# Delta-rule attention and a gelu MLP on one core: all operations but the products of zeros, in an order found anew

## The chip, the core and the metric

The kernel runs on one core of a Trainium2 chip. Five engines with queues of their own do the work: TensorE (PE, matmuls; PEld is its weight loads), VectorE (DVE), ScalarE (ACT), GpSimd (POOL), and SyncE (SP), which here only issues transfers. ACT and POOL issue some transfers too. The metric is device microseconds of one execution. The profile is one execution taken by the hardware profiler; a run's time is that of the core from start to end.

## What is computed

For 4 batches of 8 heads, a state of 48 by 48 is carried over 768 tokens; its outputs, 384 wide per token, go through an MLP with gelu:

```python
for t in range(S):                       # S = 768, B = 4, H = 8, D = 48
    kt, vt, bt = k_n[:, :, t], v[:, :, t], beta[:, :, t, None]
    y[:, :, t] = einsum('bhd,bhde->bhe', q[:, :, t], state)
    v_old = einsum('bhde,bhd->bhe', state, kt)
    state = state + bt[:, :, :, None] * einsum('bhd,bhe->bhde', kt, vt - v_old)
...
x = y.transpose(0, 2, 1, 3).reshape(3072, 384)
h = x @ w_in                             # 384 x 2048
out = gelu_tanh(h) @ w_out               # 2048 x 384
```

`k_n` is k divided by its norm plus 1e-6. Inputs and output are float32; the kernel works in bf16 with float32 accumulation.

## The kernel before, in words

**Tiling.** The sequence is cut into 12 chunks of 64 tokens. Two batches lie side by side on the 128 partitions, so a chunk has two units, numbered u = 2c and 2c + 1, each with 8 head slots. Within a chunk the recurrence is solved with matrices: a unit needs the inverse of a triangular matrix of 64 by 64 per head, and the chunk's state then goes on to the next chunk.

**Stages of a unit** (function `prep`, L469). Keys, scaled keys and queries are cast to bf16 (`kc`, `kb`, `qb`). They are transposed, on PE (`T`, `Tc`, `Tb`, `Tk`, `Tq`, evicted by `kT...`) or by a transfer that SP issues (`turn`, L510). Products of transposed keys (`GM`, `G2`, `G`, `GQ`, L521) are masked by DVE (`ln`, `wp`, L525). The inverse is found in five rounds: the start value is written into block-diagonal tiles (`X10`, `X11`), and each round i is a product `A` (L566, 8 matmuls of 128 by 128 by 64 or less), an update on DVE (`rt`, L578: two times identity plus the product), a second product `B`, and an eviction into the block-diagonal tiles. That eviction has three forms: two half copies (`bde`), a half and a scaled full copy (`bdf`), or one full copy on ACT or DVE with two half copies behind it, mostly on POOL (`xi`, then `bdc`, L608). The update has a second form: an identity product `J` on PE ahead of the accumulating product (`C`), and a plain eviction (`rj`) that ACT can do.

**Stages of a chunk** (`chain`, L611). With the state of the chunk before: `K` and `Q` (L639), `R` on DVE, `U` (the inverse times the residual, L662), its eviction `Un`, the state's update `S` and `Sn`, the output `O` (L687), its eviction `On`, and a transpose by PE (`X`, `xT`) or by a transfer (`turnx`, L704).

**The MLP of a chunk** (`mlp`, L708). 16 up products of three matmuls each (`up0` to `up15`, L716), four of them to an ACT gelu over 1024 columns (`gelu0` to `gelu3`, L720); then for each of two blocks of 128 tokens four down products of four matmuls (`down00` to `down13`, L727), an eviction (`Z0`, `Z1`) and stores (`out`, L736 and L739). The weights come in four transfers that POOL issues, `w1.0`, `w1.1` (L440), `w2.0`, `w2.1` (L442), 768 KB each.

**Products of zeros.** `warm_up` (L397) declares 70 products of 128 by 128 by 512 of a tile of zeros (`fill`, L400). Their results are read by nobody.

**What sets the order.** No scheduler runs when the kernel is built. Every operation is declared with the engines that may do it, with the buffers that it reads and writes, and with an `alt` mark where another form does the same. The text `ORDER` (L17 to L117) is one sequence over all engines; each word names an operation, behind a colon the engine (the first one declared, where none is given) and behind @ the PSUM bank. `Flow.order` (L160) cuts it into the queues of the five engines; an operation that is declared and not named is left out. `Flow.emit` (L198) puts in the waits on semaphores that the buffers need. So each engine runs its words strictly in the text's order, and a waiting word holds up all behind it on its engine. Raw q, k and v have three buffers each (`NR`), so the load of chunk c waits for the readers of chunk c - 3; the tokens' bf16 tiles have six.

Of the kernel before, what the change touches and what calls it, by code (L numbers as in the profile page):

```python
# [21 lines left out]
fill46@0 J1.1@0 fill22@1 fill64@2 Tc.1@1 fill12@2 betaT0@3 fill63@4 Tc.0@2 fill60@4 fill9@5 fill56@4 sq.0b:d sum.0a sum.0b tabS pow.0a
kTc.1:a betaA010 betaA001 pow.0b betaA011 betaA000 epsb:d eps.0a:d nsq.0a:g inv.0a eps.0b:d nsa.0b inv.0b triwpm0:d bdz0:d ib.0b:d triwpm2:d
upone0 sq.1:a sum.1 ib.0a:g kb.0:g bdz1:g kb.1:g betaT1@3 Tb.0@1 kTc.0:d betaN111 betaN110 Tb.1@4 fill25@2 kTb.0:a pow.1 eps.1:g nsa.1
kTb.1:d GM.0@6 GM.1@4 J2.0@2 fill16@1 betaN101 two:d betaN100 inv.1 ib.1:g kb.2:g ln.0 kb.3:d wpm.0 ln.1 ladj16:d wpm.1 qb.0:a fill36@3
# [4 lines left out]
X10.3:g bdc30.0:g X11.2:g qb.3:g bdf20.1:a bdf21.1:a C3.1 rj3.1:a A1.3@0 GQ.1@4 fill1@1 fill45@2 wqa.1 A4.0@1 B3.1@2 fill55@3 Tq.3@3 A1.2@4  # L30
fill41@5 rt4.0 sum.2 rt1.3 B4.0@1 wqa.0 bdf30.1:a bdf31.1:a A4.1@5 fill14@0 rt4.1 B4.1@5 fill20@0 bdf40.0:a rt1.2 pow.2 bdf41.0:a bde41.1:a
A5.0@2 B1.3@4 bde40.1:d rt5.0 kTq.3:d B1.2@0 bde10.3:a xi1.2:a R0a.0:d eps.2:g bdz5:g wqb.0 A5.1@5 B5.0@2 rt5.1 kc.4:d bde11.3:d B5.1@3
bdf50.0:a qb.2:a bdc11.2:g bdc10.2:g R0b.0:g Tq.2@5 A2.2@0 bde51.1:d rt2.2 wqb.1 nsq.2:g bde50.1:a bdf51.0:a A2.3@4 U.0@2 tabG Un.0:a rt2.3
# [4 lines left out]
gelu3.0 bdf50.3:a gelu2.0 bdf51.3:a kc.7:a down00.0@2 down01.0 sum.3 turn.5 X11.4:g wp.4 vs.1:d X10.4:d G2.5@0 S.0@6 A1.4@3 v2.01 v2.10
v2.11 q3.00 q3.01 q3.10 q3.11 k4.01 k4.10 k5.10 k4.00 k4.11 down02.0 ln.5 pow.3 eps.3:g nsq.3:g Sn.0:a bde50.2:a bde51.2:a rt1.4 inv.3 G.5@0
K.1@6 wp.5 X11.5:g X10.5:g ib.3:g kb.7:g R.1 qb.7:g B1.4@3 down10.0@4 down11.0 bde11.4:a bde10.4:a A1.5@5 GQ.2@0 A2.4@3 U.1@6 down03.0 rt1.5  # L40
rt2.4 Un.1:a wpq.2 B2.4@3 B1.5@5 xi2.4:a Q.1@6 S.1@0 O.1 down12.0 qb.6:g kb.6:g Z0.0:d bdc21.4:d bdc20.4:g A3.4@3 sq.4:g bdf10.5:a Sn.1
On.1:a turn.7 bdf11.5:a X.1@2 down13.0 xT.1:a rt3.4 sum.4 A2.5@5 B3.4@3 rt2.5 up0.1@6 up1.1 G.7@0 Z1.0:a bdf30.4:a bdf31.4:a B2.5@5 up2.1
A4.4@4 G2.7@2 up3.1 turn.6 q4.00 q4.10 q4.01 out11.0 q5.10 bde21.5:a bde20.5:a gelu0.1 wp.7 rt4.4 ln.7 up8.1@0 A3.5@5 B4.4@4 up9.1 G2.6@2
G.6@6 pow.4 eps.4:g rt3.5 ln.6 nsa.4 inv.4 ib.4:d wp.6 bdf40.4:a bdf41.4:a up10.1 B3.5@5 up11.1 up4.1@2 up5.1 A5.4@4 up6.1 bdf30.5:a
bdf31.5:a X11.7:g X10.7:g A4.5@5 A1.7@6 up7.1 X10.6:d rt5.4 X11.6:g kc.9:g q4.11 rt4.5 B5.4@7 A1.6@4 kb.8:g qb.8:g k5.11 v3.01 k5.00 k5.01
gelu2.1 kc.8:a gelu1.1 xi5.4:a v3.00 q5.01 turn.8 v4.01 v3.11 vs.2:g bdc51.4:g bdc50.4:g qb.9:g sq.5:g kb.9:g q5.11 k6.01 q5.00 turn.9 k6.00
k6.10 v3.10 k6.11 rt1.7 B4.5@5 up12.1@0 up13.1 up14.1 B1.7@2 rt1.6 B1.6@4 K.2@6 bde41.5:a bde40.5:d A5.5@5 down10.1@3 bde11.7:d rt5.5
bde11.6:a bde10.6:a bde10.7:a R.2 B5.5@5 A2.6@4 up15.1 A2.7@2 down00.1@6 bdf50.5:a bdf51.5:a gelu3.1 rt2.6 rt2.7 sum.5 B2.6@7 U.2@4
bdf20.6:a Un.2:a B2.7@2 bdf20.7:d down01.1 down11.1 bdf21.6:d bdf21.7:d down12.1 G2.8@4 Q.2@0 A3.7@2 ln.8 rt3.7 A3.6@7 O.2 On.2:a S.2@4
B3.7@2 pow.5 X11.8:g eps.5:g X10.8:g bde30.7:a bde31.7:a nsa.5 down02.1 G.8@0 rt3.6 B3.6@7 Sn.2 down03.1 bde31.6:a A4.7@2 X.2@4 wp.8 inv.5  # L50
rt4.7 A1.8@5 down13.1 rt1.8 Z0.1:a bde30.6:a xT.2:a B4.7@2 A4.6@7 Z1.1:d rt4.6 G2.9@0 G.9@4 ln.9 wp.9 B1.8@3 xi4.7:a qb.10:a ib.5:g kb.11:g
qb.11:g kc.10:d kb.10:g bdc41.7:g bdc40.7:g X11.9:g vs.3:g X10.9:g bdf10.8:a bdf11.8:a up8.2@6 B4.6@2 bde41.6:a bde40.6:a up9.2 up4.2@0
up10.2 up11.2 A5.7@4 gelu2.2 up5.2 up6.2 A5.6@5 sq.6:d rt5.6 rt5.7 sum.6 up7.2 up0.2@2 K.3@6 B5.7@4 B5.6@5 R.3 k7.01 k7.00 k7.10 out11.1
k7.11 q6.01 v4.11 turn.10 q6.10 out00.0 kc.12:g kc.11:g turn.11 sq.7:g gelu1.2 up1.2 A2.8@0 up2.2 A1.9@1 up3.2 up12.2@6 up13.2 bde50.7:d
rt2.8 rt1.9 bde51.7:a bdf50.6:a bdf51.6:a U.3@4 up14.2 B2.8@0 gelu0.2 Un.3:a B1.9@1 Q.3@2 up15.2 bde11.9:a bde21.8:a gelu3.2 pow.6 eps.6:g
nsq.6:g bde10.9:d sum.7 pow.7 kc.14:g bde20.8:a O.3 On.3:d inv.6 A2.9@1 down00.2@4 ib.6:d rt2.9 down01.2 G.10@2 G2.10@6 wp.10 ln.10 down02.2
B2.9@5 down10.2@1 A3.8@0 down11.2 G2.11@6 S.3@2 rt3.8 X11.10:g X10.10:g kb.12:g ln.11 bde20.9:a kc.13:a bde21.9:a B3.8@5 bdf30.8:a bdf31.8:a
kb.13:g X10.11:g X11.11:g A3.9@0 down12.2 down13.2 k8.00 q6.00 v4.10 q6.11 qb.12:a qb.13:g turnx.3 v4.00 k8.01 k8.11 turn.12 k8.10 rt3.9
Sn.3 A4.8@5 rt4.8 B3.9@0 A1.10@6 eps.7:g vs.4:g G.11@2 down03.2 wp.11 Z0.2:d rt1.10 Z1.2:a bdf30.9:a bdf31.9:a B4.8@5 bde41.8:a bde40.8:a
up12.3@0 up13.3 A1.11@2 A4.9@3 rt4.9 up14.3 up15.3 out11.2 q7.01 turn.13 q7.00 out00.2 v5.01 v5.10 v5.00 q7.11 v6.10 q7.10 v5.11 gelu3.3  # L60
rt1.11 up0.3@6 B1.10@3 B4.9@5 A5.8@4 up1.3 K.4@0 up2.3 up3.3 bde41.9:d rt5.8 R.4 bde40.9:a bdf10.10:a A5.9@2 bdf11.10:a up4.3@4 gelu0.3
# [729 lines left out]
```

## Time and profile before

| what | us |
|---|---|
| runs, three | 262.08, 264.64, 266.80 |
| median of the runs | 264.64 |
| the profiled execution, first to last instruction (no other time of it is listed) | 261.9 |
| PE busy in it | 243.3 |
| DVE busy | 208.7 |
| ACT busy | 189.7 |
| POOL busy | 140.6 |
| first MLP product on PE starts at | 40.08 |

The page gives the span in 40 slices of 6.5 us; a digit is the busy share in tenths. Busy PE is not PE at its peak, since matmuls overlap; what a kind of product costs is read from dense stretches of the chain, not from the mean of one.

### The profile page before, as it was taken

Reading aid. Unit: us, or ns where it says so; the run is one execution under the profiler, and the core shown is the slowest. Engines: PE = TensorE matmul, PEld = TensorE weight load, DVE = VectorE, ACT = ScalarE, POOL = GpSimd, SP = SyncE. Lnnn points to the kernel's source line nnn. Section 1 sums busy time; section 2 is a strip of 40 time slices with the busy share of each in tenths; the row PEclk is TensorE's granted clock in tenths of the full one; section 3 lists DMA queues with packets and bytes.
Section 4 is the critical chain, followed back from the end, with each engine's and each line's share of the span. In section 5 each row is a group of like instructions: output and inputs, shape, how many; then the busy total and the mean of one; then the engine's idle time right before and its main releaser. Section 6 shows DMA issues by size and latency. Waiting matters only on the chain.

```text
span 261.9 us, 12280 instructions
## 1 busy us (share of the span) xinstructions
PE 243.3 (93%) x5481; PEld 189.0 (72%) x5481; DVE 208.7 (80%) x346; ACT 189.7 (72%) x305; POOL 140.6 (54%) x216
## 2 busy tenths in 40 slices
PE   5788869999999899979999989999999999999994
PEld 1356657777878768857887877787977878878672
DVE  4699996998999999949998979799999878665100
ACT  4878886879969867947986866887847858856260
POOL 7668563687986998575165462669433522011000
PEclk9979999999999999989999999999999999999999
DMA  4869999789986988993768969568976611001422
GB/s 89 148 128 154 194 186 179 139 158 170 151 154 131 139 158 159 161 166 72 142 121 161 175 122 149 102 121 111 161 144 86 120 33 33 5 3 33 91 64 60
DMA packets 118741, 31.87 MB, mean 122 GB/s; under 512 B 112800, under 2 KB 117920, under 8 KB 118688
## 3 DMA queue, kind: packets, MB, share of 16 engines
...
q0 software_dynamic: 2880, 3.15, 7.3%
...
q14 instruction: 10, 0.08, 0.1%
...
## 4 chain that ended last, share of the span: by engine, by line
PE 75%; SPq 10%; DMA 6%; DVE 5%; issue 2%; ACT 1%
PE ps L727 24%; PE ps L716 21%; PE ps L566 18%; SPq L431 10%; DMA qraw<-in_q_dram 6%; PE ps L521 4%; PE ps L639 3%; PE ps L662 2%; PE ps L687 2%; DVE wp L525 1%; PE ps L674 1%; DVE sq L454 1%; DVE tok L484 1%; DVE rl L578 1%; SPq L406 0%
## 5 line engine op out<-in xcount | busy, mean ns | idle before, releaser
L716 PE MATMUL ps<-xT,W 128*128 128x256 bf16 x576 | 77.4, 273 | 0.4 <-ACT xT L338 0.2
L338 ACT ACTIVATE bd<-ps 64x512 bf16<-64x512 f32 x108 | 62.2, 588 | 17.6 <-PE ps L566 16.3
L727 PE MATMUL ps<-W,gT 128*128 128x384 bf16 x384 | 73.2, 329 | 0.0
L720 ACT ACTIVATE gT<-ps 128x1024 bf16<-128x1024 f32 x48 | 48.4, 1020 | 12.4 <-PE ps L716 12.0
L716 PEld LDWEIGHTS ps<-xT,W 128*128 128x128 bf16 x576 | 50.1, 98 | 6.4 <-ACT xT L338 0.5
L578 DVE TENSOR_TENSOR rt<-ps,two 128x512 bf16<-128x512 f32 x68 | 45.4, 684 | 6.6 <-PE ps L566 6.0
L727 PEld LDWEIGHTS ps<-W,gT 128*128 128x128 bf16 x384 | 33.7, 98 | 18.5 <-issue 0.7
L608 POOL COPY bd<-xi 64x256 f32<-64x256 f32 x46 | 19.0, 413 | 50.3 <-ACT xi L338 44.7
L555 POOL TENSOR_SCALAR_AFFINE_SELECT bd<-ln 64x512 bf16<-64x512 bf16 x43 | 29.7, 692 | 20.3 <-DVE ln L525 15.6
L525 DVE CAST_PREDICATED wp<-mup,ps 128x1024 bf16<-128x1024 uint16 (+1 forms) x26 | 28.3, 1090 | 2.6 <-PE ps L521 2.5
L457 POOL TENSOR_TENSOR nrm<-nrm,half 128x16 f32<-128x16 f32 x9 | 26.2, 2908 | 5.7 <-DVE nrm L455 5.5
L566 PE MATMUL ps<-rt,bd 128*128 128x64 bf16 x576 | 27.9, 194 | 0.3 <-DVE rt L578 0.3
L566 PE MATMUL ps<-wp,bd 128*128 128x64 bf16 (+1 forms) x576 | 27.3, 188 | 0.7 <-POOL bd L555 0.5
L578 DVE TENSOR_TENSOR rl<-ps,two 128x384 bf16<-128x384 f32 (+1 forms) x48 | 22.9, 483 | 5.4 <-PE ps L566 4.8
L338 DVE CAST bd<-ps 64x512 bf16<-64x512 f32 x37 | 25.0, 680 | 2.5 <-PE ps L566 2.1
L566 PEld LDWEIGHTS ps<-wp,bd 128*128 128x128 bf16 x576 | 23.6, 98 | 4.3 <-POOL bd L555 0.9
L566 PEld LDWEIGHTS ps<-rt,bd 128*128 128x128 bf16 x576 | 23.2, 98 | 4.2 <-DVE rt L578 0.8
L566 PE MATMUL ps<-rl,bd 128*128 128x64 bf16 x384 | 18.5, 193 | 2.1 <-DVE rl L578 2.1
L525 DVE CAST_PREDICATED ln<-mlo,ps 128x512 bf16<-128x512 uint16 x24 | 16.3, 682 | 4.9 <-PE ps L521 4.7
L566 PE MATMUL ps<-ln,bd 128*128 128x48 bf16 (+1 forms) x384 | 18.1, 188 | 1.0 <-DVE bd L338 1.0
L338 ACT ACTIVATE xi<-ps 128x512 bf16<-128x512 f32 x24 | 14.0, 593 | 6.5 <-PE ps L566 6.3
L566 PEld LDWEIGHTS ps<-rl,bd 128*128 128x128 bf16 x384 | 15.1, 98 | 4.8 <-DVE rl L578 3.1
...
## 6 DMA issues: line engine op xcount, KB each, us to landing
...
W<-in_moe_w_in_dram POOLq DMA_DIRECT2D x2, 768.0 KB, 10.6
W<-in_moe_w_out_dram POOLq DMA_DIRECT2D x2, 768.0 KB, 19.1
kT<-tok SPq DMA_TRANSPOSE x19, 4.5
...
```

The lines of the kernel that those rows point to most:

```text
L338: return e.activation(out, in_, ACT.Copy) if e is nc.scalar else e.tensor_copy(out, in_)
L431: lambda e, P, n=n, a=a, y=y, xs=xs, view=view: e.dma_start(raw[n][s][hf(a), :, :].rearrange("p (xg y) d -> p xg y d", y=2)[:, xs, y, :], ...
L457: if e is nc.scalar else e.tensor_tensor(nr[:, 1, hx], nr[:, 0, hx], half[:, hx], ALU.pow), reads=[nrn, "half"] + ["one", "roots"] * (c < ...
L521: ins = e.matmul(o, kT[s][r, y, g, hf(a)], kT[s][r, z, g, hf(a)])
L525: return e.copy_predicated(out.rearrange("p (x g) t -> p x g t", x=2), mask[:, 0:wd].bitcast(U16).unsqueeze(1).unsqueeze(1).to_broadcast([ ...
L555: A(("pool", "dve"), op(f"X1{a}"), lambda e, P, src=ln[m][hf(a), :, :], dst=bd[b_][hf(a), :, hf(a)], a=a: e.affine_select(out=dst, in_=src ...
L566: ins = e.matmul(P(name)[:, C * h + cs.start:C * h + cs.stop], bd[b_][:, h, :], rhs[:, h, cs], **kw)
L578: A(("dve",), op(f"rt{i}"), lambda e, P, i=i, cs=cs, cn=cn, r_=r_: e.tensor_tensor(r_[:, :, cs], P(ps(f"A{i}")).rearrange("p (h t) -> p h ...
L608: A(("pool", "dve"), op(f"bdc{i}{a}"), lambda e, P, src=xi[i_][hf(a), :, :], dst=bd[b_][hf(a), :, hf(a)]: e.tensor_copy(dst.bitcast(F32), ...
L716: ins = e.matmul(P(ph)[:, 256 * f:256 * f + 256].rearrange("p (x t) -> p x t", x=2), W1[:, j, 128 * (i + f):128 * (i + f) + 128], x_[:, :, ...
L720: A(("act",), f"gelu{i // 4}.{c}", lambda e, P, i=i, ph=ph: e.activation(g_[:, i:i + 4, :], P(ph).rearrange("p (f t) -> p f t", f=4), ACT. ...
L727: ins = e.matmul(P(po)[:, 0:DM], g_[:, f, 128 * b:128 * b + 128], W2[:, f, :], start=(f == 0), stop=(f == FC - 1))
```

## The change

Only the text `ORDER` differs. It had 1750 words and has 1701. By queue, PE had 686 and has 652, DVE 346 and 356, ACT 309 and 308, POOL 212 and 190, SP 197 and 195. The 31 words `fill...` are gone, so no product of zeros is left; the memset of their tile (`wz`) stays. All other work is there, in one of its forms, in a new sequence, with new engines and banks:

- the update with an identity product (`J`, `C`, `rj`) is used for 1 round instead of 4; `rt` for 119 instead of 116;
- the eviction by `xi` and `bdc` is used for 17 rounds instead of 30, `bde` for 64 instead of 55, `bdf` for 39 instead of 35;
- PE transposes unit 7 instead of unit 4, which is now transposed by a transfer (`turn.4`); the number of transfers of this kind stays at 19, that of `turnx` at 7;
- the masks of unit 0 and 1's query products are done by DVE (`wpq`) instead of ACT and POOL (`wqa`, `wqb`);
- the weights' four transfers, next to each other before, stand apart;
- of the four last stores two are issued by SP and two by ACT, before three and one.

The start of both texts, and the places that the prediction speaks of:

```diff
 ORDER = """
-k0x0.10:s k0x0.01:s k0x1.01:s k0x1.10:s beta00:s k1.00 k1.01 k1.10 k1.11 beta11:s q0.00 q0.01 q0.10 q0.11 v0.00 v0.01 v0.10 v0.11 wz:d
-fill23@0 tmplz:d pad0:g pad4:g tmpl0 k0x0.00:a k0x1.00:a tmpl1 fill54@1 k2.00 k2.01 k2.10 k2.11 q1.00 q1.01 q1.10 q1.11 v1.00 v1.01 v1.10
...
-qb.1:g X11.1:g fill47@6 A1.0@7 rt1.0 fill52@6 Tk.2@6 kTk.2:d B1.0@3 C1.1 w1.0 w1.1 w2.0 w2.1 GM.3@6 GM.2@4 kTq.0:a bde11.0:a bde10.0:d C2.0
...
+pad3:g half ident:g tmplz:d pad4 pad2:g one bdz5:g pad0:g tmpl0 tmpl1 triln0:d triwpm3:d epsb:g identf ladj32:d k0x0.01 pad1:g mmlo:d
+k0x0.10:a k0x1.10 k0x1.01:a k0x1.11:a two:d k0x1.00 triln1:d triwpm0:d k0x0.11 bdz0 sq.0b:d k0x0.00:a sq.0a:d mlo0 kc.1:g sum.0b sum.0a
+k1.01 beta01:a beta00:a betaT0@3 betaN000 beta10 bdz1:g k1.11 betaN010 betaN011 tabS pow.0b pow.0a k1.00 eps.0b betaN001 k1.10 k2.01 k2.00
...
+GM.1@4 ln.1 X11.1 triwpm1 nsa.1 inv.1 betaT1@0 sq.2 sum.2 triln3 betaA100 betaA101 betaA111 A1.0@1 rt1.0 B1.0@1 q1.10 betaA110 ib.1 ladj16
...
+q2.10 k3.00 bdz2:g q2.11 Tq.2@5 Tq.3@4 kTq.3 k3.11 GQ.0@6 B3.1@0 X10.3 kTq.2 w1.0 bdf30.1 k4.00 A4.0@1 rt4.0 bdf31.1 q4.10 GM.2@2 ln.2 X11.3
+A1.3@4 rt1.3 q2.01 B4.0@1 bde41.0 A4.1@0 rt4.1 kb.4:g bde40.0 wpm.2 k4.10 Tq.1@5 B1.3@4 w1.1 X10.2 B4.1@0 bdf40.1 A5.0@1 X11.2 A1.2@2 rt5.0
...
+v1.11 up2.0 up3.0 v1.10 triwpm4 bdf31.3:d wpq.3 B3.2@0 A4.3@1 rt4.3 up4.0@6 qb.4:g turn.4 qb.5:g tabG gelu2.0 w2.0 up12.0@4 up13.0 up5.0
...
+up7.11 up14.11 up15.11 down00.11@0 down10.11@1 gelu1.11 down01.11 down02.11 gelu3.11 out00.10 down03.11 down11.11 down12.11 down13.11 Z1.11
+Z0.11:d out01.11 out00.11 out10.11:a out11.11:a
 """
```

More of the change, by code (lines that the diff above doesn't have):

```diff
@@ L22 @@
[L22 to L25, printed above, removed]
@@ L30 @@
[L30 to L33, printed above, removed]
@@ L38 @@
[L38 to L61, printed above, removed]
@@ L70 @@
-up10.4 A2.13@0 up11.4 gelu3.4 G2.14@2 rt2.13 ln.14 gelu2.4 B5.11@6 B2.13@7 bde51.11:a bde21.13:a bde50.11:a G.14@0 G2.15@2 bde20.13:d ln.15
-wp.14 up0.4@4 up1.4 up2.4 B3.12@2 up3.4 U.5@6 A3.13@3 up4.4@0 up5.4 up6.4 up7.4 gelu0.4 xi3.12:d rt3.13 inv.8 X11.15:d X11.14:g X10.15:g
-X10.14:g A1.14@3 B3.13@2 rt1.14 bde31.13:d Un.5:a Q.5@6 gelu1.4 S.5@4 O.5 G.15@0 bdc31.12:g bdc30.12:g ib.8:g kb.17:g out11.3 q8.10 v6.01
-v7.10 v6.00 q8.00 q8.11 k10.00 q9.01 k9.10 k9.01 k9.11 v7.00 bde30.13:a qb.17:a turn.17 On.5:a Sn.5 wp.15 down00.4@3 A4.13@2 down01.4
@@ L82 @@
-A3.15@0 K.7@2 A4.14@1 up14.5 up15.5 up0.6@4 rt3.15 kc.19:d R.7 A1.16@0 up1.6 up2.6 up3.6 A1.17@2 B3.15@3 gelu3.5 xi3.15:a rt1.16 B1.16@0
-rt4.14 B4.14@1 down00.5@6 rt1.17 B1.17@7 down01.5 bdf40.14:a bdf41.14:a xi1.16:a sq.10:g bdc31.15:d bdc11.16:g bdc10.16:g bdc30.15:d sum.10
-A4.15@1 A5.14@3 down02.5 down03.5 rt5.14 bde10.17:d B5.14@0 A2.16@3 down10.5@2 down11.5 k11.10 kc.22:g pow.10 qb.19:g gelu0.6 bde11.17:a
-bdf50.14:a bdf51.14:a rt2.16 rt4.15 B2.16@3 bde20.16:d Z0.5:d bde21.16:a B4.15@1 down12.5 A2.17@0 bde41.15:a bde40.15:a turn.18 q10.00
@@ new lines @@
+down13.0 Z1.0 B2.5@0 bde21.5 bde20.5:d q4.11 B3.4@3 up0.1@1 up1.1 k5.11 turn.6 G2.6@4 bde30.4 kc.8:g ln.6 bde31.4 G.7@6 up2.1 up3.1 q4.00
+q4.01 qb.9:a up8.1@4 up9.1 A4.4@0 wp.7 up10.1 up11.1 A3.5@3 qb.8:g gelu0.1 rt4.4 gelu2.1 rt3.5 B4.4@0 bde41.4:d bde40.4 v2.00 up4.1@6 up5.1
+B3.5@1 bdf30.5 X10.6 G.6@2 wp.6 up12.1@4 bdf31.5 q5.00 A5.4@0 rt5.4 up6.1 up7.1 A4.5@1 rt4.5 k5.00 gelu1.1 k5.10 X11.6 q5.01 A1.6@2 A1.7@3
+q6.11 B5.4@0 bde51.4 up13.1 B4.5@1 bdf40.5 up14.1 v4.10 rt1.6 B1.6@2 kb.9:g bde50.4:d q6.00 rt1.7 down00.1@6 sq.5:g sum.5 kc.11:g turn.8
@@ new lines @@
+ib.5:g v5.10 kb.11:g X.2@4 B4.6@5 xi4.6 down03.1 bdc40.6 rt4.7 B4.7@0 bde41.7 xT.2:d up4.2@4 up5.2 up6.2 up7.2 k7.11 gelu1.2 rt1.8 B1.8@1
+bde11.8 q6.10 bdc41.6:d A5.6@7 out00.0 bde40.7:d A5.7@0 rt5.7 v4.00 up0.2@2 up1.2 G.9@4 rt5.6 k6.10 bde10.8:d B5.6@7 up2.2 xi5.6 up8.2@0
+up3.2 up9.2 up10.2 A2.8@7 v4.01 up11.2 v3.11 kb.10:g v4.11 wp.9 sq.6 X10.9 vs.3 turn.10 gelu0.2 kc.13 sum.6 k8.11 v5.00 rt2.8 X11.9 A1.9@4
+k8.00 qb.11:g turn.11 gelu2.2 Z0.1 k8.10 k8.01 rt1.9 B5.7@5 bde50.7 bde51.7 k7.01 bdc51.6 down10.2@2 down00.2@3 B1.9@4 bdf10.9 k7.00 bdf11.9
@@ new lines @@
+up13.4 up14.4 up15.4 bde10.13 gelu3.4 A5.10@5 bdf21.12:d turn.14 up8.4@0 up9.4 up10.4 rt5.10 B5.10@4 bde51.10 kb.15:g turn.15 bde11.13:d
+K.5@6 up11.4 down13.3 bde50.10:d A2.13@3 bdc41.11 Z1.3 R.5 v8.01 rt2.13 bdc40.11 A5.11@4 up0.4@6 out00.2 vs.6 v8.11 out00.3 rt5.11 A3.12@2
+rt3.12 gelu2.4 up1.4 B2.13@3 bde21.13 G2.14@4 G2.15@0 ln.15 X11.15 ln.14 bde20.13 up2.4 X10.15:d inv.8 B5.11@2 bdf50.11 up3.4 gelu0.4 X11.14
+G.14@0 A3.13@3 rt3.13 q10.00 up4.4@4 up5.4 up6.4 up7.4 wp.14 B3.13@3 bdf51.11 U.5@6 down00.4@2 q10.11 k9.11 Un.5:d X10.14 A1.14@0 rt1.14
@@ new lines @@
+vs.9 R.9 Z1.7:d up4.8@0 up5.8 up6.8 rt5.18 B5.18@2 bdf10.20 bdf11.20 up7.8 gelu2.8 bde51.18 bde50.18 A2.20@6 up0.8@4 up1.8 gelu1.8 X11.21
+bdf40.19:d bdf41.19:d A5.19@7 q11.10 out11.6 kb.23:g A1.21@3 up2.8 up3.8 rt2.20 B2.20@2 gelu0.8 up12.8@0 rt1.21 B1.21@3 rt5.19 B5.19@6
+bde20.20:d up13.8 up14.8 xi5.19 up15.8 bde21.20:d A3.20@2 bde10.21 qb.22:g turn.22 G2.22@4 G.22@6 bde11.21:d gelu3.8 qb.23:g turn.23 rt3.20
+down00.8@3 ln.22 bdc50.19 bdc51.19 A2.21@2 U.9@0 Un.9 wp.22 X10.22 X11.22:d B3.20@4 xi3.20 bdc31.20:d down01.8 G2.23@6 ln.23 Q.9@0 O.9 On.9
```

122 lines of the change are left out of this document (66 added, 56 removed).

## The prediction

> **What bounds the kernel now.** I read the profile's page first (engine sums, the 40 slices, the shares of the chain that ended last), then busy time by windows, then the timelines of TensorE and of the two DMA-issuing queues.
>
> ```profile
> span 261.9 us, 12280 instructions
> PE 243.3 (93%) x5481; PEld 189.0 (72%) x5481; DVE 208.7 (80%) x346; ACT 189.7 (72%) x305; POOL 140.6 (54%) x216
> PE   5788869999999899979999989999999999999994
> PEclk9979999999999999989999999999999999999999
> PE 75%; SPq 10%; DMA 6%; DVE 5%; issue 2%; ACT 1%
> ```
>
> The reader is to see two stages. In the first six slices PE is at 5 to 8 tenths; from the seventh on it is at 9 nearly throughout, and the chain lies on PE for 75% of the span.
>
> ```profile
> 18.86:40.08 21.22, 16.60 (x427) 12.35 (x425) 19.56 (x38) 17.60 (x31) 14.62 (x25) 1.00 1.10 177
> 40.08:258.30 218.22, 213.13 (x4924) 170.11 (x4924) 176.00 (x274) 158.85 (x249) 112.80 (x154) 0.99 0.67 117
> ...
> 40.08 0.50 PE L716 MATMUL ps<-xT,W 128*128 128x256 bf16 x3 [0.22 <-ACT xT L338]
> ...
> 18.86 0.68 DVE L578 TENSOR_TENSOR rt<-ps,two 128x512 bf16<-128x512 f32 x1
> ```
>
> The columns of a window are its length, then busy PE, weight loads, DVE, ACT and POOL, then granted clock, DMA share and GB/s. Between the first update of an inverse (`rt1.0`, 18.86) and the first MLP product (`up0.0`, 40.08) DVE is the fullest engine, 19.56 of 21.22 us; after 40.08 PE is busy 213.13 of 218.22 us.
>
> How much of the second stage is work that no order can shorten? The cost of each kind in a dense stretch stands in the chain:
>
> ```profile
> 60.43 0.47 PE ps L566 x16
> ...
> 64.65 0.47 PE ps L521 x32
> ...
> 248.00 5.24 PE ps L716 x48
> 253.24 5.21 PE ps L727 x32
> ```
>
> An up product of 3 matmuls is 0.327 us, a down product of 4 is 0.651, an A or B product of 8 is 0.235, a set of 32 small matmuls 0.47. After `up0.0` there stand 192 ups (62.8), 96 downs (62.5), 209 A and B products (49.1), 40 grams of 16 (9.4), 44 sets of 32 for K, Q, S and O (20.7; I price them all by the gram's row), 11 U of 16 matmuls (5.2) and some 2.5 for transposes and rest: 212.2 us. The stage took 218.2, so 6.0 us at most can be won in it.
>
> ```profile
> 114.28 0.22 PE L687 MATMUL ps<-us,wp 64*64 64x48 bf16 x4 [1.71 <-issue]
> 151.74 0.21 PE L687 MATMUL ps<-us,wp 64*64 64x48 bf16 x3 [1.05 <-issue]
> ```
>
> Of these 6.0, 2.8 are two stops in the middle of an operation with no producer to blame, and about 2 more the half clock that followed the first (below). An order has no handle on them.
>
> **The change, part by part.** The order text lists what each queue runs; nothing else differs.
>
> *PE's work after the first MLP product.* Counted in the new order, the same kinds stand behind `up0.0` in the same numbers: 192, 96, 209, 40, 44, 11. The term is 212.2 in both, so it costs nothing and gains nothing. DVE has 273 operations behind that point before and 277 now; it is no fuller either.
>
> *The 31 products of zeros and three of four identity products go.*
>
> ```profile
> L400 PE MATMUL ps<-wz 128*128 128x512 bf16 x31 | 13.4, 497 | 1.4 <-DVE wz L350 1.2 <-DVE rt L578 0.2
> ```
>
> At the warm spacing (5.21 us over 32 matmuls of 384 columns gives 0.163, so about 0.217 for 512 columns) they are 6.7 us of PE, all ahead of `up0.0`, where PE waits anyway: no gain by itself. What covers this is that PE was idle or filling for more than 6.7 us there. What they gave was the clock.
>
> ```profile
> 14.38 1.07 PE L521 MATMUL ps<-kT 48*64 48x64 bf16 x64
> 20.52 0.75 PE L521 MATMUL ps<-kT 48*64 48x64 bf16 x64
> ...
> 108.91 0.40 PE L566 MATMUL ps<-rt,bd 128*128 128x64 bf16 x8
> 117.71 0.63 PE L566 MATMUL ps<-wp,bd 128*128 128x64 bf16 x8
> ...
> 12.00:14.00 2.00, 0.97 (x9) 0.57 (x8) 1.97 (x6) 0.81 (x2) 1.47 (x3) 0.83 0.80 144
> 14.00:16.00 2.00, 2.00 (x67) 1.22 (x67) 1.97 (x9) 1.97 (x4) 0.58 (x2) 0.50 0.72 133
> 116.00:117.00 1.00, 1.00 (x26) 0.57 (x18) 0.56 (x2) 0.69 (x2) 0.31 (x1) 0.50 0.75 146
> ```
>
> The granted clock was 0.50 in 14 to 16 and in 116 to 117 us, the first time after PE had worked 0.97 of 2 us, the second after the stop of 1.71 us above. At that clock 64 gram matmuls 1.07 instead of 0.75, a product of 8 takes 0.63 instead of 0.40. In the new order PE has 12.9 us of work (by the costs above) between the first A product and `up0.0`, some 22 us: a density of 59%, not far over 0.97 of 2. If the clock stays half there, the path to the first pair's inverses pays 10 products (2.3 us), a gram (0.3), U, O and two transposes (about 0.8 by the same ratio), and the first ups run at half rate until the gate opens (in 14 to 17 us this took about 3 us of full PE, so some 1.6 us): 5.0 in all. If it stays full: 0, and below 0 only by the fills' own places, which held nothing up. I take 2.5, the middle, because 59% lies between the 49% that lost the clock and the 78% (16.60 of 21.22) that kept it.
>
> The Trainium skill ("TensorE: Matmul & The Clock Gate", section "Why this matters for your kernels") says the half rate returns after one idle window of about 3 us without matmuls. By that rule the new order, which has no such gap after the first grams, would keep the clock and this term would be 0. The trace does not quite agree: a stop of 1.71 us amid thin work was enough at 112 to 116 us.
>
> *The start.* Loads of the first keys are spread over SP and ACT as before; the square-root table now comes first on ACT.
>
> ```profile
> 7.12 1.00 DVE L455 TENSOR_REDUCE nrm<-sq 128x8 f32<-128x384 f32 x2
> 8.86 0.21 ACT L456 ACTIVATE nrm<-nrm 128x8 f32<-128x8 f32 x1
> ```
>
> The sums ended at 8.12 and the root began at 8.86, so at most 0.7 us (and about as much from scaling the first keys on DVE) is won; without fills the first gram, at half clock like before's, gains nothing more, and the transposes ahead of it may lose the little they had of the full clock. I put `rt1.0` at 18.2, 0.7 earlier (bounds 17.4 and 18.9).
>
> *DVE from there to `up0.0`.* By the groups' means (0.684 for a full update, 0.669 and 0.682 for masks, 0.680 for an eviction, and so on) the old order has 36 operations worth 21.8 us there, which took 21.2. The new has 39 worth 22.9: two more updates (the identity products' evictions went from ACT back to DVE), one mask more, fewer evictions. At the same ratio 22.3 us, as DVE stays the fullest engine. So `up0.0` comes at 18.2 + 22.3 = 40.5 with a full clock, 43.0 with the clock term: +2.9 against 40.08.
>
> *The weights.* This is moved on POOL's queue.
>
> ```profile
> 21.85 1.78 POOL L442 DMA_DIRECT2D W<-in_moe_w_out_dram  x2
> ...
> 22.06 12.67 SPq L431 DMA_DIRECT2D qraw<-in_q_dram  x4
> ...
> 28.97 15.54 DMA qraw<-in_q_dram
> ...
> W<-in_moe_w_in_dram POOLq DMA_DIRECT2D x2, 768.0 KB, 10.6
> W<-in_moe_w_out_dram POOLq DMA_DIRECT2D x2, 768.0 KB, 19.1
> ```
>
> Before, all four halves were issued by 23.6 us (w_out's last), and what SP issued behind them crawled: four q loads took 12.67 us to issue, and one landed 15.54 us after its turn, which delayed the transposes of unit 4 to 45.2. Now `w1.0` and `w1.1` stand 13.7 and 10.6 us of DVE work ahead of `up0.0`, against 10.6 us to land: just in time, no term. But `w2.0` stands behind the casts `qb.4`, `qb.5`, which need q2, which SP issues behind `k4.00` and `q4.10`, and these wait for POOL to finish with k1 and q1. Its place is 3.4 us of PE work after `up0.0`, and `down00.0`, which reads it, 6.65 after: 3.2 us of cover if POOL is no further than its place, 10.3 if it runs ahead as far as its last wait (`bdc11.3`, 6.6 us of DVE work before `up0.0`) allows. Against 10.6 to land, PE waits 0.3 to 7.4 us; with 19.1 it would be more. I take 2.4, nearer to the low end, as POOL was busy only 14.62 of 21.22 us in that stage. The spread loads free SP for q2 and v1 in return; PE no longer does unit 4's transposes but unit 7's, the same work.
>
> *The end.* The last four stores: two on SP and two on ACT, where the two issues follow each other, instead of three and one. One issue more on the path is 0.55.
>
> **Sum** against the profiled execution: 261.9 + 2.9 + 2.4 + 0.55 = 267.75, which is +2.2%. Its span lies just under the fastest of the three runs (262.08); their median is 264.64. On the median's scale I forecast 264.64 + 5.85 = 270.5 us.
>
> **Rivals.** (1) *The clock holds and the weights come in time*: +0.4 for the start and 0.55 for the end give 265.6, within 2%. For it: no gap of 3 us in the new PE queue, and POOL mostly idle. Against it: the 0.50 rows. (2) *Faster*: the start gains (`rt1.0` at 17.4, `up0.0` at 39.6), and the 6.0 us lost after 40.08 vanish, since the stops and the half clock at 112 to 119 us do not come back. Worked out: 264.64 - 0.5 - 6.0 + 0.55 = 258.7; with the end's 0.55 hidden, 258.1. It decides if PE never waits after `up0.0`; for it speaks that the work per engine is equal there, against it that stops without a producer appeared twice in 262 us. (3) *The loads fall behind*: w2 lands at 19.1 us as before, and the transposes by DMA (turn.4 and turn.5, queued on SP behind v1) crawl with it: a wait of 19.1 - 10.3 = 8.8 instead of 2.4, and the full clock loss of 5.0: 270.5 + 6.4 + 2.5 = 279.4. For it: the 15.54 row. Against it: only one half is under way at a time.
>
> **How the numbers follow.** Forecast case 0.42, rival (1) 0.32, faster 0.18, loads behind 0.08. About 2% (5.3 us, near the 4.7 us between the runs of before) is what a measurement can tell from no change, so faster means under 259.3 and slower over 269.9. The forecast case's own range, 267 to 275, reaches a little under the bound, and the edge of rival (1) a little over 2%; the two cancel. Faster 0.19, same 0.32, slower 0.49. The range takes in both neighbours and leaves one in ten at either side: 258 to 279.
>
> **What would show it.** Right: no L400 group; PEclk at 5 or 6 tenths in slices 2 to 6; the first L716 row at 42 to 44 us; an idle entry of L727 released by W's DMA of 1 to 5 us; PE at 9 from then on. Wrong: a full clock from 18 us on with `up0.0` at 40 or earlier; W2 landed before the first L727; or idle entries of PE after 60 us released by DVE, POOL or by kT's transposes, which would mean that the later order, which I priced at nothing, carries a term of its own.

## The result, and the profile after

The changed kernel takes 278.16 us (median of four runs, 274.88 to 280.0) against 264.73 us (262.08 to 266.8) for the kernel before beside it: a ratio of 1.049, 95% interval 1.0388 to 1.0593. It is 13.4 us slower; the forecast was 5.85 us slower. Ratios here leave disturbed executions out, so they need not be the ratio of the medians. In the code after, every line from the middle on stands 8 higher (L716 is L708, L727 is L719, L566 is L558).

The page of the changed kernel, its rows of span, engine sums, TensorE's slices and clock, and shares of the chain:

```profile
span 277.0 us, 12168 instructions
PE 244.2 (88%) x5447; PEld 193.8 (70%) x5447; DVE 210.6 (76%) x356; ACT 189.2 (68%) x301; POOL 133.8 (48%) x194
PE   0578779689999889998999996999899999999994
PEclk9999968889999999997999999999999999999998
PE 50%; DMA 17%; SPq 12%; DVE 8%; POOL 7%; issue 2%; ACT 2%; POOLq 0%
```

All engines have about the busy time that they had. But TensorE carries 50% of the chain, not 75%, and transfers with SP's issues 29%, not 16%. There are thin slices behind the first up product, the 6 at 48 to 55 us and the 6 at 166 to 173 us. The two stages by windows, and three stretches of the second:

```profile
16.09:42.40 26.31, 20.97 (x439) 18.04 (x440) 20.77 (x38) 18.77 (x33) 19.92 (x33) 0.88 0.91 153
42.40:273.10 230.70, 217.63 (x4912) 171.42 (x4909) 177.29 (x279) 161.40 (x249) 105.26 (x135) 0.98 0.66 110
42.00:60.00 18.00, 15.14 (x303) 11.61 (x301) 11.75 (x21) 9.78 (x14) 9.23 (x12) 0.87 1.32 151
60.00:140.00 80.00, 75.03 (x1828) 59.73 (x1827) 69.53 (x108) 61.77 (x101) 52.14 (x66) 0.98 0.77 130
140.00:255.00 115.00, 109.94 (x2608) 87.96 (x2605) 95.09 (x152) 82.63 (x128) 44.28 (x58) 1.00 0.55 98
```

The same three stretches of the kernel before:

```profile
42.00:60.00 18.00, 17.50 (x476) 13.70 (x475) 16.35 (x26) 14.12 (x23) 11.59 (x16) 1.00 0.93 158
60.00:140.00 80.00, 77.32 (x1938) 62.12 (x1937) 72.50 (x111) 63.95 (x106) 56.95 (x73) 0.98 0.82 145
140.00:255.00 115.00, 113.09 (x2473) 90.83 (x2472) 85.93 (x136) 79.66 (x121) 43.19 (x63) 1.00 0.53 93
```

The profiled executions differ by 277.0 - 261.9 = 15.1 us. The first up product comes 42.40 - 40.08 = 2.3 later. From there to TensorE's end it takes 230.7 instead of 218.2: 12.5 us more for the same products. Of these, TensorE's idle time is 13.1 instead of 5.1, so 8.0; and it is busy 217.6 instead of 213.1, so 4.5. About half of the 4.5 is a lower granted clock: by the stretches above, 18 x 0.13 + 80 x 0.02 = 3.9 us are lost to it after and 80 x 0.02 = 1.6 before. No run here shows where the rest comes from. The end takes 0.3 more. What TensorE waits for from 42.4 us on, in total, times, and the longest, after:

```profile
PE ps L558 <- POOL bd L547: 4.5, 2, 2.7
PE ps L513 <- DMA kT<-tok: 2.5, 1, 2.5
PE ps L558 <- issue: 1.5, 2, 1.1
PE ps L558 <- ACT bd L330: 1.4, 2, 1.0
...
PE ps L719 <- DMA W<-in_moe_w_out_dram: 0.3, 1, 0.3
```

and before, from 40.08 us on:

```profile
PE ps L687 <- issue: 2.8, 2, 1.7
PE ps L566 <- DVE rl L578: 1.0, 1, 1.0
```

Seven microseconds lie in three stops, two on POOL's start values (`X11`) and one on a transposed key tile. In TensorE's timeline, behind the row of the first up products, they are:

```profile
42.40 3.15 PE L708 MATMUL ps<-xT,W 128*128 128x256 bf16 x24
...
53.36 0.64 PE L513 MATMUL ps<-kT 48*64 48x128 bf16 x16 [2.52 <-DMA kT<-tok]
...
98.14 0.41 PE L558 MATMUL ps<-wp,bd 128*128 128x64 bf16 x8 [1.80 <-POOL bd L547]
...
171.38 0.64 PE L558 MATMUL ps<-wp,bd 128*128 128x64 bf16 x16 [2.66 <-POOL bd L547]
```

POOL itself was idle until just before. Its timeline at these two places:

```profile
95.80 1.48 POOL L641 TENSOR_TENSOR vraw<-vraw,nrm 128x768 f32<-128x768 f32 x1 [3.63 <-DMA vraw<-in_v_dram]
97.42 0.66 POOL L547 TENSOR_SCALAR_AFFINE_SELECT bd<-ln 64x512 bf16<-64x512 bf16 x1
...
169.05 1.47 POOL L446 TENSOR_TENSOR sq<-kraw 128x768 f32<-128x768 f32 x1 [3.84 <-DMA kraw<-in_k_dram]
170.66 1.45 POOL L547 TENSOR_SCALAR_AFFINE_SELECT bd<-ln 64x512 bf16<-64x512 bf16 x2
```

The word ahead of `X11.9` on POOL is `vs.3` (the values of chunk 3 scaled), the one ahead of `X11.16` is `sq.11` (squares of chunk 11's keys). Each waits 3.6 to 3.8 us for a load, and TensorE waits for the start value behind it. In the new order these two loads stand right ahead of their readers, and each engine runs its words in the order of the text. That was to be seen in the text before the run: between v3's last load and its reader stood 14.4 us of TensorE's work (at the forecast's costs) in the old order and none in the new; for k11 it was 2.5 us and none at the same costs.

SP's queue at 27 to 43 us, after:

```profile
27.61 9.63 SPq L423 DMA_DIRECT2D vraw<-in_v_dram  x4
38.05 4.83 SPq L502 DMA_TRANSPOSE kT<-tok  x2
```

`turn.4` and `turn.5` are issued behind four value loads that took 9.63 us to issue, and while w_out is on its way they take 8.1 and 12.3 us from issue to landing; the page's median over all 19 is 5.2. The stop of 2.52 us ends when the later of the two has landed.

### The profile page after: what moved, and what is told of

Read it like the earlier page. It is cut to its first block, busy times and chain, and to the rows that moved or that the text cites. A ratio compares the mean times of both kernels' runs of the same rounds, so it can differ in the third digit from the quotient of the medians.

```text
span 277.0 us, 12168 instructions
## 1 busy us (share of the span) xinstructions
PE 244.2 (88%) x5447; PEld 193.8 (70%) x5447; DVE 210.6 (76%) x356; ACT 189.2 (68%) x301; POOL 133.8 (48%) x194
## 4 chain that ended last, share of the span: by engine, by line
PE 50%; DMA 17%; SPq 12%; DVE 8%; POOL 7%; issue 2%; ACT 2%; POOLq 0%
PE ps L719 17%; PE ps L708 14%; PE ps L558 12%; SPq L423 10%; DMA kraw<-in_k_dram 6%; DMA W<-in_moe_w_out_dram 5%; DMA qraw<-in_q_dram 4%; POOL nrm L449 2%; PE ps L631 2%; PE ps L513 2%; DVE nrm L447 2%; DMA vraw<-in_v_dram 1%; ACT bd L330 1%; POOL tok L330 1%; DVE wp L517 1%
## 5 line engine op out<-in xcount | busy, mean ns | idle before, releaser
L330 ACT ACTIVATE bd<-ps 64x512 bf16<-64x512 f32 x120 | 69.5, 589 | 27.9 <-PE ps L558 26.5
L719 PE MATMUL ps<-W,gT 128*128 128x384 bf16 x384 | 76.2, 332 | 0.3 <-DMA W<-in_moe_w_out_dram 0.3
L708 PE MATMUL ps<-xT,W 128*128 128x256 bf16 x576 | 76.5, 273 | 0.0
L570 DVE TENSOR_TENSOR rt<-ps,two 128x512 bf16<-128x512 f32 x71 | 48.0, 683 | 11.0 <-PE ps L558 10.1
L708 PEld LDWEIGHTS ps<-xT,W 128*128 128x128 bf16 x576 | 50.9, 98 | 6.9 <-DVE ln L517 0.2
L719 PEld LDWEIGHTS ps<-W,gT 128*128 128x128 bf16 x384 | 33.6, 99 | 17.8 <-issue 1.4
L558 PE MATMUL ps<-wp,bd 128*128 128x64 bf16 (+1 forms) x576 | 28.6, 192 | 8.1 <-POOL bd L547 5.4
L330 DVE CAST bd<-ps 64x512 bf16<-64x512 f32 x47 | 31.9, 681 | 3.7 <-PE ps L558 3.1
L558 PE MATMUL ps<-rt,bd 128*128 128x64 bf16 x576 | 30.5, 200 | 2.8 <-DVE rt L570 2.4
L558 PEld LDWEIGHTS ps<-wp,bd 128*128 128x128 bf16 x576 | 23.9, 100 | 12.9 <-POOL bd L547 5.3
L600 POOL COPY bd<-xi 64x256 f32<-64x256 f32 x26 | 11.3, 433 | 40.1 <-ACT xi L330 30.2
L558 PEld LDWEIGHTS ps<-rt,bd 128*128 128x128 bf16 x576 | 25.0, 102 | 7.6 <-DVE rt L570 4.3
L336 ACT ACTIVATE bd<-ps,up 128x512 bf16<-128x512 f32 x32 | 21.5, 673 | 0.7 <-DVE bd L330 0.6
L558 PE MATMUL ps<-ln,bd 128*128 128x48 bf16 (+1 forms) x384 | 19.2, 193 | 3.1 <-DVE bd L600 1.6
L641 POOL TENSOR_TENSOR vraw<-vraw,nrm 128x768 f32<-128x768 f32 x10 | 14.8, 1478 | 14.5 <-DMA vraw<-in_v_dram 14.2
L558 PEld LDWEIGHTS ps<-ln,bd 128*128 128x128 bf16 x384 | 16.0, 101 | 5.9 <-DVE bd L600 1.7
L513 PE MATMUL ps<-kT 48*64 48x64 bf16 (+1 forms) x832 | 17.7, 216 | 2.7 <-DMA kT<-tok 2.5
## 6 DMA issues: line engine op xcount, KB each, us to landing
W<-in_moe_w_out_dram POOLq DMA_DIRECT2D x2, 768.0 KB, 12.5
```

What stands on the lines that cost most here:

```text
L330: return e.activation(out, in_, ACT.Copy) if e is nc.scalar else e.tensor_copy(out, in_)
L336: return e.activation(out, in_, ACT.Copy, scale=up1[:, 0:1]) if e is nc.scalar else e.tensor_scalar(out, in_, up1[:, 0:1], None, op0=ALU.mult)
L513: ins = e.matmul(o, kT[s][r, y, g, hf(a)], kT[s][r, z, g, hf(a)])
L558: ins = e.matmul(P(name)[:, C * h + cs.start:C * h + cs.stop], bd[b_][:, h, :], rhs[:, h, cs], **kw)
L570: A(("dve",), op(f"rt{i}"), lambda e, P, i=i, cs=cs, cn=cn, r_=r_: e.tensor_tensor(r_[:, :, cs], P(ps(f"A{i}")).rearrange("p (h t) -> p h ...
L708: ins = e.matmul(P(ph)[:, 256 * f:256 * f + 256].rearrange("p (x t) -> p x t", x=2), W1[:, j, 128 * (i + f):128 * (i + f) + 128], x_[:, :, ...
```

## The experiments

**Theory:** the extra loss lies behind the first up product, in words that wait for a transfer at the head of their engine's queue and hold up what stands behind them: start values behind `vs.3` and `sq.11` on POOL, transposes by transfer behind loads on SP. **Rival A:** it is the clock, which the products of zeros held. **Rival B:** it is w_out's late halves, and all that crawls with them. Times are medians; every ratio is against runs of the kernel before beside it.

| kernel | us | before | ratio (95%) |
|---|---|---|---|
| swap | 273.15 | 265.19 | 1.041 (1.030 to 1.052) |
| wearly | 275.23 | 265.19 | 1.038 (1.019 to 1.057) |
| fills | 275.01 | 265.19 | 1.036 (1.012 to 1.059) |
| nofill | 267.33 | 265.19 | 1.017 (1.002 to 1.031) |
| swapfills | 276.32 | 264.83 | 1.037 (1.025 to 1.049) |
| loads2 | 278.94 | 264.83 | none |
| three | 271.47 | 264.83 | 1.026 (1.018 to 1.034) |
| hoist | 292.47 | 264.83 | 1.105 (1.096 to 1.115) |
| pe45 | 269.91 | 266.01 | 1.017 (1.010 to 1.024) |
| edf | 274.40 | 266.01 | 1.032 (1.023 to 1.041) |
| three45 | 273.26 | 266.01 | 1.028 (1.022 to 1.033) |
| all | 273.10 | 266.01 | 1.029 (1.022 to 1.035) |
| bturn4 | 269.52 | 267.21 | 1.023 (1.013 to 1.033) |
| pe45fills | 271.24 | 267.21 | 1.031 (1.020 to 1.043) |

The changed kernel itself has 1.049 (1.039 to 1.059). three, pe45, three45 and all lie clear below that, and hoist clear above. swap, wearly, fills, swapfills and edf overlap with it and with one another, so their times do not rank the causes; what each of them took away is read from its profile.

**POOL's two words (swap).** In the new order, only this (parts of two lines):

```diff
-wp.9 sq.6 X10.9 vs.3 turn.10 gelu0.2 kc.13 sum.6 k8.11 v5.00 rt2.8 X11.9 A1.9@4
+wp.9 sq.6 X10.9 turn.10 gelu0.2 kc.13 sum.6 k8.11 v5.00 rt2.8 X11.9 vs.3 A1.9@4
...
-rt4.14 sq.11:g sum.11 X11.16 A1.16@6
+rt4.14 X11.16 sq.11:g sum.11 A1.16@6
```

> The changed order with two words moved on POOL: the scaling vs.3 goes behind the start value X11.9, the square sq.11 behind X11.16. Theory Q (POOL's queue): in the changed kernel's profile PE idles 1.80 and 2.66 us for a start value that stands on POOL behind an operation that waits for a load; both idle entries go, and the time falls by 3 to 4.5 us, to 274 to 275. Theory C (clock and start alone carry the loss): the two waits are slack that returns elsewhere, under 1 us.

It took 273.15, so by the medians 8.0 over before instead of 13.4, or 5.4 us given back, a little more than Theory Q had; by the ratios it is 0.8%, within the intervals. In the profile the two stops on POOL, 4.5 us, are gone from the list, and TensorE ends at 267.3 instead of 273.1. The stop on the transfer stays:

```profile
52.12 0.55 PE L513 MATMUL ps<-kT 48*64 48x128 bf16 x16 [1.94 <-DMA kT<-tok]
```

**w_out's halves early (wearly).** `w2.0 w2.1` right behind `w1.1`, as before.

> The changed order with w2.0 and w2.1 moved to stand right behind w1.1 on POOL. Theory W (the late weights and the transfers they collide with carry the loss at 50 to 60 us, where PE idles 2.9 us and runs at half clock from 53 to 57): the wait of 2.5 us for kT and the half clock after it go, 3 to 5 us gained. Rival: the same bytes then starve q2 and v1 earlier, the casts of unit 4 come later, and the time is within 1.5 us of the changed kernel or above it.

It is 10.0 over before instead of 13.4, with an interval that tells it neither from the changed kernel nor from swap. No wait for w_out is left, but the wait for the transposes is (2.27 us, which Theory W said would go), and so are the POOL stops (3.6 us in two). In the changed kernel's profile the wait for w_out itself was 0.35 us. So Rival B is not shown to hold much of the loss; its price is open within the interval.

**Products of zeros back (fills), and out of the kernel before (nofill).** The 31 words in places like their old ones in the new order; and the old order without them.

> The changed order with 31 products of zeros put back (8 at the start, 3 to 1 at a time ahead of PE's waits up to the third unit's products). Theory C (the half clock costs): the granted rate is full from about 14 us, up0.0 starts at 39.5 to 41 instead of 42.4, and the time falls by 2 to 4 us. Rival D (DVE and the loads set the start): up0.0 stays within 0.7 us of 42.4 and the time within 1 us of the changed kernel.

> The kernel before without its 31 products of zeros, all else in place. Theory C: half rate until the MLP starts, up0.0 at 42 to 43 instead of 40.08, time +2 to +3.5 us against before. Rival D: DVE was the fullest engine there and covers the slower products, so up0.0 moves less than 1 us and the time stays within 1 us.

In the old order they are worth 2.1 us by the medians (the ratio allows 0.2 to 3.1%), and the first up product comes at 41.71 without them instead of 40.08. In the new order it comes at 39.22 with them, 3.2 earlier, and the time is 9.8 over before instead of 13.4, within an interval 4.7% wide; its runs took 270.41 to 279.73, and the profile is of the one with 270.41. In TensorE's timeline of fills:

```profile
39.22 2.78 PE L710 MATMUL ps<-xT,W 128*128 128x256 bf16 x24
55.44 1.46 PE L721 MATMUL ps<-W,gT 128*128 128x384 bf16 x4 [3.14 <-DMA W<-in_moe_w_out_dram]
```

TensorE, earlier, now meets the second half of w_out 3.14 us before it has landed. Rival A explains 2 to 4 us by the medians, not the 13.4. The same profile shows something else: from 42 us on it has no wait for the transposes and only one of 0.7 us for POOL's start values, although `vs.3` and `sq.11` stand ahead of the start values as in the changed kernel. There `vs.3` waits 0.85 us for its load instead of 3.63. So the two stops on POOL are not fixed by the order alone; the order puts a waiting word ahead of the start value, and how late the load lands sets the price.

**Both (swapfills); with early weights as well (three).**

> The changed order with both the swap on POOL and the 31 products of zeros. If the two costs are separate: 278.2 - 5.0 - 3.2 = 270. If an earlier start only runs into the late weights (in the run with the fills alone PE waited 3.14 us for the second half of w_out): 272 to 274.

> Swap, fills, and w2.0, w2.1 right behind w1.1. If clock, POOL's queue and the late weights are the change's loss: 278.2 - 5.0 - 3.2 - 3.0 = 267, PE without a wait for w_out and up0.0 at 39 to 40.5. If the early weights starve q2 and v1 instead: 270 or more.

Neither adds up. swapfills, at 276.32, lies above both of its ranges; it has 1.64 us of wait for w_out and 3.06 for the transposes, and is no faster than fills. three is at 271.47, in the second of its ranges, and its wait for the transposes is 4.45 us at 52.45. What is won ahead of a late transfer can be lost at it, but how much is not shown, since the same wait differs by 3 us without a changed word (loads2, below).

**Loads moved instead of their readers: two chunks' (loads2), all later ones up to 60 words earlier (hoist), all in the order of their readers (edf).** loads2 puts v3's loads behind `v2.00` and k11's behind `kc.16`; edf puts the loads of q, k and v into the same places of SP's queue, sorted by first reader; hoist is three with the later loads moved up.

> The changed order with eight words moved on SP alone: the four loads of v3 go to stand behind v2.00 (v3.11 stood behind loads of v4 and v5), the four of k11 behind kc.16. POOL's order stays. Theory Q1 (what POOL waits for is a load that SP issues too late): the idle entries of 1.80 and 2.66 us go as they did with the swap, and the time falls to 273 to 275 from 278. Theory Q2 (only POOL's order matters, the loads come late for want of bandwidth): no gain, 277 to 279.

> The one before, and every load of q, k and v behind up0.0 moved up to 60 words earlier, as far as its buffer's readers allow. If late loads still hold POOL and DVE: 1 to 3 us less than with the three edits, 264 to 266, level with the kernel before. If SP's queue, which has to wait in order, now blocks its transposes: slower than the three edits.

> The changed order with the loads of q, k and v permuted among their own places in the text, so that the one whose reader comes first goes first; nothing else moves. Theory Q1 (late loads hold POOL's squares and scalings, and start values behind them): the idle entries for POOL go and the time falls by 3 to 6 us, to 272 to 275. Rival (the order among loads is not what is late): 277 to 280.

In loads2 and edf the stops on POOL's start values go as in swap, and TensorE's wait for the transposes is longer. In loads2, and in edf:

```profile
56.73 0.64 PE L513 MATMUL ps<-kT 48*64 48x128 bf16 x16 [5.66 <-DMA kT<-tok]
```

```profile
55.22 0.64 PE L513 MATMUL ps<-kT 48*64 48x128 bf16 x16 [4.54 <-DMA kT<-tok]
```

In loads2 no word ahead of that place differs from the changed kernel, where the wait was 2.52 us: 3 us of it come and go by themselves. Its four runs took 274.48 to 280.56, so whether it gains is open. edf, at 274.40, lies in the range of its Theory Q1 and about where swap does. hoist is the worst of all, 27.6 us over before; TensorE waits eight times for transposes:

```profile
PE ps L515 <- DMA kT<-tok: 21.0, 8, 7.3
```

The longest of the eight is not a slow transfer: it landed 4.0 us after its issue, but SP, with the loads moved ahead of it, issued it at 50.85, where the changed kernel issues its first two from 38.05 on. So moving all loads up is wrong as a cure. The loads and the transposes share SP's queue, and what is put first makes the other late.

**Transposes of units 4 and 5 on TensorE (pe45).** swap, and this (parts of lines; `up12.0` and `up13.0` move too):

```diff
-up4.0@6 qb.4:g turn.4 qb.5:g tabG gelu2.0 w2.0 up12.0@4 up13.0 up5.0
-triwpm5:g bde31.2 B4.3@1 bde30.2:d A4.2@0 rt4.2 up14.0
+up4.0@6 qb.4:g qb.5:g tabG gelu2.0 T.4@4 kT.4:d w2.0 up5.0
+triwpm5:g bde31.2 B4.3@1 bde30.2:d A4.2@0 rt4.2 up12.0@4 up13.0 up14.0
...
-kc.5:g turn.5
+kc.5:g T.5@4 kT.5:d
```

> The changed order with the swap on POOL, and units 4 and 5 transposed by PE (T, kT on DVE) instead of by the transfers turn.4 and turn.5; up12.0 and up13.0 go behind A4.2 to cover the eviction. Theory K (transposes by transfer crawl behind the weights and loads: PE idled 2.5 us for kT near 50 us and then ran at half clock to 57): the wait and the half clock go, 2 to 4 us less than the swap alone (273.2), against 1.3 us more PE and 1.9 more DVE work: 270 to 272. Rival: the stage waits for k, q or v anyway, 273 or more.

It took 269.91, 3.9 over before: by the medians 4.1 more given back than by swap, and the intervals (1.010 to 1.024 against 1.030 to 1.052) lie apart. It is the best of the new order's versions. It was not run without the swap on POOL, nor with `up12.0` and `up13.0` in their old places. The page's chain lies on TensorE for 76% again. No transposed tile is waited for from 42 us on, and the half clock behind that wait is gone (granted 0.81 in swap, 1.00 here):

```profile
42.00:60.00 18.00, 14.92 (x335) 11.56 (x333) 12.94 (x22) 10.73 (x16) 10.17 (x14) 1.00 0.89 143
60.00:140.00 80.00, 77.77 (x1942) 62.99 (x1943) 74.09 (x115) 65.06 (x105) 53.13 (x67) 1.00 0.80 134
140.00:255.00 115.00, 112.34 (x2588) 88.85 (x2588) 89.44 (x142) 80.36 (x123) 42.03 (x55) 1.00 0.56 95
```

From 60 us to its end TensorE is idle for 4.9 us here and 4.6 before. What is left of idle time lies in 42 to 60, where TensorE is busy for 17.50 - 14.92 = 2.6 us less than before. There it waits for DVE, no longer for a transfer. TensorE also makes the transposes of units 5 and 7 here, which the kernel before leaves to transfers, 0.67 us each in its timeline. The two waits are:

```profile
46.62 0.37 PE L558 MATMUL ps<-ln,bd 128*128 128x48 bf16 x8 [1.08 <-DVE bd L330]
...
52.14 0.36 PE L558 MATMUL ps<-wp,bd 128*128 128x32 bf16 x8 [1.47 <-DVE bd L336]
```

The second of these is of my making: DVE takes `kT.5` ahead of that eviction, and `kT.5` waits for TensorE's transposes, as DVE's timeline shows:

```profile
50.38 0.96 DVE L330 COPY kT<-ps 128x1536 bf16<-128x1536 bf16 x1 [2.79 <-PE ps L485]
```

**The same replacement alone, in the kernel before (bturn4).** `T.4` and `kT.4` out, `turn.4` in the place of `T.4`.

> The kernel before, with unit 4's six tiles transposed by the transfer turn.4 instead of by TensorE (T.4 and kT.4), in the same places of the sequence; nothing else is changed. Theory (a transpose by transfer in the stretch from 42 to 60 us is itself the cost, in whatever order it stands): TensorE gets an idle entry of 2 us or more released by the transfer of kT in that stretch, and the time is 3 to 5 us above before (ratio 1.011 to 1.019). Rival (the transfer is harmless in the old order, and only the new order's loads around it make it late): no such idle entry over 1 us, ratio 0.996 to 1.004.

It took 269.52 against 267.21, 2.3 us more by the medians, and has the stop that the theory asked for, in the old order:

```profile
49.16 0.86 PE L521 MATMUL ps<-kT 48*64 48x64 bf16 x32 [2.27 <-DMA kT<-tok]
```

The clock follows: in 42 to 60 it was granted 0.81, before 1.00. The theory had 3 to 5 us: the medians lie a little under that, the ratio over it, so the stop is shown and its price only roughly. The transfer did not crawl here: it landed 3.9 us after its issue. It was issued late, at 45.19, since the query cast ahead of it waited for a load that landed 17.3 us after its turn; the kernel before has that cast too, but goes on from it on TensorE and DVE. So a transfer of ordinary length is enough for a stop where its tile is ready late and needed at once.

**pe45 with more (three45: three and pe45, with `T.4` later, behind `gelu0.0`; all: three45 and the sorted loads; pe45fills: pe45 and the products of zeros).**

> Swap, fills, early w2 (the run with three edits, 271.5) and units 4 and 5 transposed by PE. That run's one large idle entry was 4.45 us for kT. Theory K: it goes, and 3 to 5 us with it: 266.5 to 268.5. Rival: under 1.5 us gained.

> The one before with the loads permuted as well, by first reader. If late loads still cost there: 264 to 267, level with the kernel before. If they do not: as without the permutation.

> The best kernel so far (start values ahead of the waiting POOL words, units 4 and 5 transposed by TensorE) with the 31 products of zeros put back in the places that they had in the earlier run of products of zeros; w2.0 and w2.1 stay at their places. Theory (start, POOL's order and transposes are separate terms): the first up product at 38.5 to 39.5 instead of 40.4, and 2 to 3 us less than 269.9, so a ratio of 1.006 to 1.010. Rival (every microsecond won ahead of the first up product is waited for at the next late load, as in the runs of products of zeros before): TensorE waits longer for w_out's weights or for a cast whose load is late, between 46 and 56 us, and the ratio stays at 1.014 to 1.020.

None is better than pe45. three45 has no wait for a transfer left, where three had 4.45 us for the transposes, and is no faster (1.028 and 1.026), as its rival had it; so the transposes' price holds for the step from swap to pe45 and not everywhere. all has no wait for POOL or a transfer from 42 us on, and still 273.1; its stops are without a producer (the longest 1.28, 1.12, 1.12 and 0.37 us) or on DVE. pe45fills has its first up product at 38.29, 2.1 earlier than pe45, and is by the medians as far over before (4.0 and 3.9); its ratio, 1.031, lies above both ranges that were stated for it. One stretch of it:

```profile
42.00:60.00 18.00, 14.27 (x304) 10.39 (x302) 12.31 (x20) 9.57 (x15) 10.73 (x14) 0.91 0.99 156
```

From its first up product to TensorE's end it takes 227.5 us, and pe45 takes 223.6. Of the 3.9 more, 1.2 are idle and 2.6 busy, part of them at a lower clock (granted 0.91 here, 1.00 in pe45). So what was won at the start is lost behind it, as the rival for this run had it, but not at a late load: the stops of 42 to 60 us are the same as in pe45, on DVE and ACT. Why the clock was lower is open. No version beat the kernel before.

## Why the prediction was wrong, point by point

**The failed step: "The term is 212.2 in both, so it costs nothing and gains nothing."** The count was right; the conclusion was not. The same products took 12.5 us longer, 8.0 idle and 4.5 busy, about half of this at a lower clock. I had compared how much stands on each engine, not what stands ahead of what, and so put the later order at nothing. Two pieces were found and taken away. POOL's two words were 4.5 us of stops in the profile and 5.4 us by the medians, a step that the intervals alone do not confirm. The transposes of units 4 and 5 by transfer were 4.1 us by the medians, with the half clock that follows, a step that the intervals do confirm. Both together bring the ratio from 1.049 to 1.017, clear of the noise. "PE no longer does unit 4's transposes but unit 7's, the same work" belongs to this step: bturn4 shows that it was not the same for unit 4, where the transfer alone gave a stop of 2.27 us. Of the 13.4 us, 3.9 stay over in pe45. In its profile, which is 6.0 us longer than that of before, TensorE is busy 2.6 us less in the stretch from 42 to 60 us. How much of that is the new order and how much the place that I gave `kT.5` is open.

**The clock, +2.5 (bounds 0 to 5).** The size was fair: nofill gives 2.1 in time by the medians and 1.6 at the first up product, though at this place 2 us differ between runs of one order (last section). The half rate came as bounded, though not as a continuous stretch. Products of 8 matmuls in the timeline after:

```profile
27.35 0.61 PE L558 MATMUL ps<-rt,bd 128*128 128x64 bf16 x8
...
30.25 0.41 PE L558 MATMUL ps<-rt,bd 128*128 128x64 bf16 x8
...
37.94 0.61 PE L558 MATMUL ps<-rt,bd 128*128 128x64 bf16 x8
```

0.61 is the half clock by the rows of before (0.63 against 0.40). It lasted to 29 us, opened, and closed again. By windows after:

```profile
32.00:34.00 2.00, 0.99 (x28) 0.77 (x27) 1.83 (x4) 1.66 (x4) 1.52 (x5) 1.00 1.18 223
34.00:36.00 2.00, 0.93 (x32) 0.72 (x32) 1.83 (x4) 1.95 (x4) 1.67 (x3) 1.00 1.09 195
36.00:38.00 2.00, 1.31 (x26) 1.18 (x27) 1.90 (x4) 0.56 (x2) 0.82 (x3) 0.58 0.86 167
```

TensorE was busy 0.99 and 0.93 of 2 us, stopped for 1.61, and the clock went to 0.5. The rule of the Trainium skill ("TensorE: Matmul & The Clock Gate", section "Why this matters for your kernels"), one idle window of about 3 us, would have given no half clock here; this trace does not agree. The forecast's other row was read wrongly in one word: the stop of 1.71 us at 112 us in the kernel before did not stand amid thin work, as TensorE was busy for the whole of each microsecond from 108 to 112.

**The start.** `rt1.0` came at 16.09, not 18.2, ahead of my lower bound of 17.4. But then 26.31 us went by to the first up product, where I had 24.8 (22.3 of DVE and 2.5 of clock). DVE was busy for only 20.77 of them, so it did not set the length as it had before. The first up product at 42.40 (I had 43.0) is thus right by luck: one term was 2.1 too late, the other 1.5 too short.

**The weights, +2.4 (0.3 to 7.4).** 0.35 us at 58.52, the low end. In the chain after:

```profile
38.48 0.88 POOL W L434
...
44.14 14.34 DMA W<-in_moe_w_out_dram
```

The first half was issued 3.9 us ahead of the first up product and some 11 ahead of the first down product, at 49.53: POOL ran ahead of its place, as the far end of my range for the cover (10.3) had it, though the forecast does not show how 10.3 follows from its 6.6 and 6.65. The second half took 14.34 us; TensorE, held up by the transposes, came to it hardly earlier. In the versions where it came earlier it paid 1.64 and 3.14, so the term was hidden, not absent.

**The end, +0.55.** 0.3 in the profile: right, and small.

**The rivals.** "The loads fall behind" gave 279.4 and had 0.08: time and mechanism (`turn.4` and `turn.5` crawling on SP) were nearest to the result, but it put the price on w_out and the clock at the start, and missed POOL. The forecast's last paragraph named a sign that would refute it, idle entries after 60 us released by DVE, POOL or kT's transposes. POOL's are there, at 98.14 and 171.38; the one for kT is at 53.36, ahead of the 60 us.
